# The opening of an attention and feed-forward kernel in one written order

## The chip, the cores and the metric

The kernel runs on one core of one Trainium2 chip. The metric is the device time of one execution in microseconds; the figure for a kernel is the median of its runs. The names of the engines are those of the profile: PE is TensorE, DVE is VectorE, ACT is ScalarE, POOL is GpSimd, and SP is the queue from which the kernel issues its DMAs.

## What is computed

An attention over 4 batches, 8 heads, 768 positions and 64 dimensions of a head, with a local window (96 positions) and 8 global keys, followed by a gated feed-forward part on 3072 tokens. Cut to what matters:

```python
scores = (1 / sqrt(D)) * q @ k.T
keep = is_global | is_local                     # pos < 8, or 0 <= rel < 96
scores = where(keep, scores - slopes * dist, -1e9)
a = softmax(scores)
x = reshape(a @ v)                              # 3072 x 512
h = ((x @ w1) * (x @ w2)) @ w3                  # w1, w2: 512 x 1024; w3: 1024 x 1024
return (h @ w_out).astype(float32)              # w_out: 1024 x 512
```

The four weights are float64 in memory.

## The kernel before

**The product of the two last weights.** Since nothing stands between `w3` and `w_out`, the kernel multiplies them once, at its start: the product, 1024 x 512, has eight row blocks f = 0 to 7 of 128 rows, and each is a sum over eight k of a matmul of a 128 x 128 block of `w3` (transposed, from `w3t`) with row block k of `w_out` (L96). `fold` does this.

**Converting the weights.** A float64 weight comes in pieces of 128 x 512 numbers (512 KB). `words` (L45) loads one piece as pairs of 32-bit words into a raw buffer, and three DVE operations (L53, L54, L55) shift and join the words into float32. There are 40 pieces: 8 of `w_out` (tile `wo`), 16 of `w3t` (tiles `t3_f_z`, two halves z of each row block f; the profile calls them `t`), and 16 of `w1` and `w2` (tile `t3s`). The pieces for the product take turns in four raw buffers `stage` (L82), those of `w1` and `w2` in two, `raws` (L132). In the text below t_f_z, o_k and w_k are these pieces, in that order.

**Two parts of a number.** Where PE is to multiply with nearly float32 accuracy, a matrix is split into a high part and a low part (`split`, L58): ACT copies x into a tile of the type float32r, and a subtraction gives x minus that copy. For the activations DVE subtracts; for `w1`, `w2` (L139) and for the product of the weights (L101) GpSimd does. `done` (L98) first copies a finished row block of the product from PSUM to `wf`, then splits `wf` into `wh` and `wl`.

**The steps.** The attention has 24 steps `s`; each takes two pairs of heads of a block of 256 queries. A step on PE has the values of the step before (L435, L437), the scores (L392), and four `flip`s, transposes of the probabilities (L423, L425). `softmax` (L395) has the fused bias, maximum and subtraction on DVE (L407), the exponential on ACT (L408), a sum and reciprocal on DVE (L409, L410), and the scaling, of one head of a pair on ACT (L413) and of the other on DVE (L414). The transposed probabilities are copied out of PSUM by ACT (L427). `split` at L482 takes a step's result into `xh` and `xl`, the input of the feed-forward part. `biases` makes the masks and distances; `bias` scales them for two heads.

**What sets the order.** The order on PE is written out (`manual_schedule`, L459); on the other engines and on SP a planner chooses. Feed-forward work (`run`, L142) and the product of the weights (`fold`, L86) are generators, cut into slices, which PE does between the flips: `SLICES` says how many stand ahead of each flip of a step. `fold` has 16 slices (L119: row blocks 2 to 7 in turn, after 0 and 1 together), so that with `FIRST` the steps 0 to 3 hold the product and one slice more, and the feed-forward part begins at the end of step 3. `ins` (L129) converts `w1` and `w2`, 1, 4, 4, 4 and 3 pieces ahead of the steps 0 to 4 (`INS`, L447).

PE's order on one step, as written:

```python
for m in range(STEP * NQ):
    slices(SLICES[s][m])
    phs.append(flip(*pairs(s)[m // NQ], m % NQ, prs[m // NQ]))
slices(SLICES[s][-1])
```

The product's accumulators are in the pool `ps_m` (two buffers), those of the values in `ps_v` (one), those of the flips in `ps_t` (one).

Of the kernel before, what the change touches and what calls it, by code (L numbers as in the profile page):

```python
# [20 lines left out]
P = 128  # L21
# [23 lines left out]
def words(nc, raw, dst, src):  # L45

    if src.dtype == F32:
        nc.sync.dma_start(out=dst, in_=src.bitcast(I32))
        return
    nc.sync.dma_start(out=raw, in_=src.bitcast(I32))  # L50
    w = raw.rearrange("p (n t) -> p n t", t=2)

    nc.vector.tensor_scalar(out=dst, in0=w[:, :, 1], scalar1=3, scalar2=0x3FFFFFF8, op0=ALU.logical_shift_left, op1=ALU.bitwise_and)  # L53
    nc.vector.scalar_tensor_tensor(out=dst, in0=w[:, :, 1], scalar=-0x40000000, in1=dst, op0=ALU.bitwise_and, op1=ALU.bitwise_or)  # L54
    nc.vector.scalar_tensor_tensor(out=dst, in0=w[:, :, 0], scalar=29, in1=dst, op0=ALU.logical_shift_right, op1=ALU.bitwise_or)  # L55


def split(nc, hi, lo, x, eng=None):  # L58

    nc.scalar.activation(hi, x, AF.Copy)  # L60
    (eng or nc.vector).tensor_tensor(out=lo, in0=x, in1=hi.bitcast(F32), op=ALU.subtract)  # L61


class FeedForward:
# [3 lines left out]
    def __init__(self, ctx, tc, w1, w2, w3t, w_out, out):  # L68
        self.nc = tc.nc
        self.src = (w1, w2)  # L70
        self.w3t, self.w_out, self.out = w3t, w_out, out
        self.wp = wp = ctx.enter_context(tc.tile_pool(name="wp", bufs=1))
        self.mp = ctx.enter_context(tc.tile_pool(name="mp", bufs=2))
        self.ps = ctx.enter_context(tc.tile_pool(name="ps_m", bufs=2, space=PSUM))
        self.w = [[wp.tile([P, NFC, NCC, P], F32R, name=f"w{n}{x}") for x in "hl"] for n in (1, 2)]
        self.wh, self.wl = (wp.tile([P, NFC, DO], F32R, name=n) for n in ("wh", "wl"))

        self.wo = self.mp.tile([P, NFC, DO], I32, tag="gh", bufs=1, name="wo")
        self.stage = self.mp.tile([P, 4, 2 * PC], I32, tag="gl", bufs=1, name="stage")
        self.turn = 0  # L80

    def staged(self, dst, src):  # L82
        words(self.nc, self.stage[:, self.turn % 4], dst, src)
        self.turn += 1

    def fold(self):  # L86
        nc = self.nc
        t3 = {}

        def piece(f, z):  # L90
            t3[f] = self.mp.tile([P, PC], I32, tag="ag"[z], name=f"t3_{f}_{z}")
            self.staged(t3[f], self.w3t[f, :, z * PC:(z + 1) * PC])

        def product(ps, f, k):
            z, i = divmod(k, HF)
            nc.tensor.matmul(ps, lhsT=t3[f][:, i * P:(i + 1) * P].bitcast(F32), rhs=self.wo[:, k].bitcast(F32), start=k == 0, stop=k == NFC - 1)  # L96

        def done(ps, f):  # L98
            full = self.mp.tile([P, DO], F32, tag="o", name=f"wf_{f}")
            nc.scalar.activation(full, ps, AF.Copy)  # L100
            split(nc, self.wh[:, f], self.wl[:, f], full, eng=nc.gpsimd)  # L101


        ps = [self.ps.tile([P, 512], F32, tag="m", name=f"w_{f}") for f in range(2)]
        for k in range(NFC):
            z, i = divmod(k, HF)
            if i == 0:
                piece(0, z)
            self.staged(self.wo[:, k], self.w_out[k])
            product(ps[0], 0, k)  # L110
            if i == 0:
                piece(1, z)
            product(ps[1], 1, k)
            if k == NFC - 1:
                for f in range(2):
                    done(ps[f], f)
            if k % 2:
                yield
        for f in range(2, NFC):  # L119
            ps = self.ps.tile([P, 512], F32, tag="m", name=f"w_{f}")  # L120
            for z in range(2):
                piece(f, z)
                for i in range(HF):
                    product(ps, f, HF * z + i)
                if z == 1:
                    done(ps, f)
                yield

    def ins(self, xp):  # L129
        nc = self.nc  # L130

        raws = xp.tile([P, 2, 2 * PC], I32, tag="xl", name="raws")  # L132
        t3s = xp.tile([P, 4, PC], I32, tag="xh", name="t3s")
        for k in range(2 * NFC):
            f, n = divmod(k, 2)
            t3 = t3s[:, k % 4]
            words(nc, raws[:, k % 2], t3, self.src[n][f])
            x = t3.bitcast(F32).rearrange("p (i m) -> p i m", i=NCC)
            split(nc, self.w[n][0][:, f], self.w[n][1][:, f], x, eng=nc.gpsimd)  # L139
            yield  # L140
# [42 lines left out]
def attention_moe(ctx: ExitStack, tc: tile.TileContext, qk, vx, w1, w2, w3t, w_out, ns, out):  # L183
# [3 lines left out]
    nt = cp.tile([P, 4], I32, name="nt")  # L187
    nc.sync.dma_start(out=nt, in_=ns.bitcast(I32).partition_broadcast(P))
    ident = cp.tile([P, P], F32, name="ident")
    make_identity(nc, ident)  # L190
    nf = cp.tile([P, 4], F32, name="nf")
    nc.vector.tensor_copy(out=nf, in_=nt)
    ff = FeedForward(ctx, tc, w1, w2, w3t, w_out, out)
    banded(tc, ff, nf, ident, qk, vx)

    okt = cp.tile([P, 6], F32, name="okt")
    for i, (c, s, op) in enumerate(((0, 0.0, ALU.is_ge), (0, float(GLB), ALU.is_le), (2, 1.0, ALU.is_ge), (2, float(WIN), ALU.is_le), (1, 0.0, ALU.is_equal), (3, 0.0, ALU.is_equal))):
        nc.vector.tensor_scalar(out=okt[:, i:i + 1], in0=nf[:, c:c + 1], scalar1=s, scalar2=None, op0=op)
    okm = cp.tile([P, 1], F32, name="okm")
    nc.vector.tensor_reduce(out=okm, in_=okt, axis=mybir.AxisListType.X, op=ALU.min)  # L200
    oki = cp.tile([P, 1], I32, name="oki")
    nc.vector.tensor_copy(out=oki, in_=okm)
# [113 lines left out]

@with_exitstack
def banded(ctx, tc, ff, nf, ident, qk, vx):
# [17 lines left out]
    def biases():  # L336
# [13 lines left out]
        nc.vector.tensor_scalar(out=loc, in0=rel, scalar1=0.0, scalar2=None, op0=ALU.is_ge)  # L350
        nc.vector.scalar_tensor_tensor(out=loc, in0=rel, scalar=nl, in1=loc, op0=ALU.is_lt, op1=ALU.mult)
# [21 lines left out]
    def load(c, hp):  # L373
        b, cb = divmod(c, NCB)
        k0 = 0 if cb else BW
        nw = 2 * NQ if cb else 2 * NQ - 1
        qr = ld.tile([P, QW], F32, tag="qr", name=f"qr_{c}_{hp}")
        vr = ld.tile([P, 2 * NQ, 2 * D], F32, tag="vr", bufs=2 * STEP, name=f"vr_{c}_{hp}")
        nc.sync.dma_start(out=qr[:, k0:], in_=qk[b, cb, hp, :, k0:])
        nc.sync.dma_start(out=vr[:, :nw], in_=vx[b, cb, hp, :, :nw])  # L380
        return qr, vr

    def scores(c, hp, t):
# [11 lines left out]
    def softmax(c, hp, ps):  # L395
# [4 lines left out]
        for j in range(NQ):  # L400
            first = c % NCB == 0 and j == 0
            w0 = BW if first else 0
            for u in range(2):
# [4 lines left out]
                nc.scalar.activation(pr[:, j, u, w0:], pr[:, j, u, w0:], AF.Exp, bias=m, scale=-1.0, accum_out=sm[:, j, u:u + 1])  # L408
        nc.vector.tensor_scalar(out=sm, in0=sm, scalar1=1e-9, scalar2=None, op0=ALU.add)  # L409
        nc.vector.reciprocal(out=sm, in_=sm)  # L410
        for j in range(NQ):
            w0 = BW if c % NCB == 0 and j == 0 else 0
            nc.scalar.activation(pr[:, j, 0, w0:], pr[:, j, 0, w0:], AF.Copy, scale=sm[:, j, 0:1])  # L413
            nc.vector.tensor_scalar(out=pr[:, j, 1, w0:], in0=pr[:, j, 1, w0:], scalar1=sm[:, j, 1:2], scalar2=None, op0=ALU.mult)  # L414
# [15 lines left out]
    def values(uu, c, hp, t, phs):  # L430
        for j, ph in enumerate(phs):
            first = c % NCB == 0 and j == 0
            for u in range(2):
                rows, o = slice(u * D, (u + 1) * D), uu[u * D:(u + 1) * D, j * P:(j + 1) * P]
                nc.tensor.matmul(o, lhsT=t[1][:, j, rows], rhs=ph[:, u, 0], start=True, stop=first)  # L435
                if not first:
                    nc.tensor.matmul(o, lhsT=t[1][:BW, 2 * NQ - 1 - j, rows], rhs=ph[:BW, u, 1], start=False, stop=True)  # L437
# [6 lines left out]

    FIRST = 1
    SLICES = [(2, 1, 1, 0, 0)] * 4 + [(5, 2, 2, 2, 1)] * (n - 4)
    INS = [1, 4, 4, 4, 3]  # L447
# [8 lines left out]
    work.append(ff.fold())  # L456
    more = ff.ins(xp)
    phs, vals = [], []
    with tc.manual_schedule(engines={mybir.EngineType.PE}):  # L459
        ts = [load(*pairs(0)[0])]  # L460
        slices(FIRST)
        dists = biases()
        ts += [load(*p) for p in pairs(0)[1:]]
        for s in range(n + 1):
            for _ in range(INS[s] if s < len(INS) else 0):
                next(more, None)
            if s < NP // STEP:
                for _, hp in pairs(s):
                    bias(hp, *dists)
            if s:  # L470
                c, h0 = pairs(s - 1)[0]
                if h0 == 0 and c % 2 == 0:
                    xs = [xp.tile([P, NCC, W], F32R, tag=tag, name=f"{tag}_{c}") for tag in ("xh", "xl")]
                xc = [x[:, :, c % 2 * T:][:, :, :T] for x in xs]
                uu = ps_v.tile([P, STEP, T], F32, tag="v", name=f"v_{c}_{h0}")
                for i, p in enumerate(pairs(s - 1)):
                    values(uu[:, i], *p, vals[i], phs[NQ * i:NQ * (i + 1)])
            if s < n:
                ps = [scores(*p, t) for p, t in zip(pairs(s), ts)]
            if s:  # L480
                hs = slice(h0, h0 + STEP)
                split(nc, xc[0][:, hs], xc[1][:, hs], uu)  # L482
# [61 lines left out]
```

## Time and profile before

| | us |
|---|---|
| median of 3 runs | 644.0 (643.03 to 644.11) |
| the profiled execution | 642.88 |
| its span, first to last instruction | 641.0 |
| PE busy in the span | 595.4 |
| ACT busy | 288.7 |
| DVE busy | 270.2 |
| POOL busy | 37.4 |

The span is what the views of the trace divide; the profiled execution's own time has 1.9 us around it. A row of a view of time gives the start, the length, the engine, the line, the operation, what is written and read, the count, and in brackets the idle time ahead of it with what ended it. A row of windows gives a stretch, its length, the busy time of PE, of PE's weight loads, of DVE, of ACT and of POOL with the number of instructions, then the granted clock of PE, the busy share of the DMA engines, and GB/s. A row of waits says who waited for whom, the total, how often, and the longest. A row of DMA issues ends with KB of one and the median time from issue to landing.

### The profile page before, as it was taken

What the parts mean: (1) busy time and instruction counts of PE and PEld (TensorE: products, weight loads), DVE (VectorE), ACT (ScalarE), POOL (GpSimd) and SP (SyncE); (2) the same over time, 40 slices, a digit from 0 to 9 for tenths busy, and PEclk for the clock granted to TensorE, in tenths of its full rate; (3) what the DMA queues carried; (4) which work ended last, traced back from release to release, by engine and by line L of the source; (5) the groups of instructions that cost most, each with busy time, mean ns of one, the idle gap of its engine ahead of it and who ended that gap; (6) DMA issues with size and microseconds to landing.
All of it is one profiled execution on the core that took longest, in us unless ns stands there. A gap on an engine that the chain in (4) does not pass through costs nothing.

```text
span 641.0 us, 9165 instructions
## 1 busy us (share of the span) xinstructions
PE 595.4 (93%) x3488; PEld 466.7 (73%) x3488; DVE 270.2 (42%) x839; ACT 288.7 (45%) x769; POOL 37.4 (6%) x34
## 2 busy tenths in 40 slices
PE   3678695999999999999999999999999999999996
PEld 1234444698898888888778888888888888888884
DVE  6999999234223333430444233334313442312210
ACT  0625364555345545643555355455525654522210
POOL 0033543200000000000000000000000000000000
PEclk9799797999999999999999999999999999999999
DMA  8768654102202210221122032101221220000001
GB/s 321 260 242 303 205 178 138 43 33 59 92 1 90 91 48 26 74 75 50 59 74 74 4 113 97 42 17 59 91 84 39 74 74 1 34 33 1 0 18 53
DMA packets 23237, 53.96 MB, mean 84 GB/s; under 512 B 2704, under 2 KB 4752, under 8 KB 23184
## 3 DMA queue, kind: packets, MB, share of 16 engines
q1 hardware_dynamic: 23184, 53.29, 25.0%
q8 instruction: 29, 0.48, 0.3%
q14 instruction: 24, 0.20, 0.1%
HBM read 46.99 MB, written 6.29 MB: 83 GB/s over the span
## 4 chain that ended last, share of the span: by engine, by line
PE 79%; DVE 12%; ACT 5%; issue 2%; DMA 2%; POOL 0%; SPq 0%; DVEq 0%; ACTq 0%
PE m L154 14%; PE m L156 13%; PE m L155 13%; PE o L171 7%; PE o L173 7%; PE o L172 7%; PE s L392 4%; PE v L435 4%; ACT pr L408 3%; PE t L423 3%; PE v L437 3%; PE t L425 3%; DVE t L54 2%; PE w L96 2%; DMA stage<-w3t 2%
## 5 line engine op out<-in xcount | busy, mean ns | idle before, releaser
L427 ACT ACTIVATE ph<-t 128x512 f32<-128x512 f32 (+1 forms) x96 | 53.8, 560 | 103.4 <-PE t L425 89.1
L408 ACT ACTIVATE pr<-pr,mx 128x232 f32<-128x232 f32 (+1 forms) x192 | 88.4, 462 | 24.6 <-DVE mx L407 24.6
L164 DVE TENSOR_TENSOR g<-m,a 128x512 f32<-128x512 f32 x48 | 33.1, 690 | 135.4 <-PE m L156 135.4
L154 PE MATMUL m<-xh,w1h 128*128 128x512 f32 (+1 forms) x224 | 85.2, 380 | 1.4 <-ACT a L161 1.4
L154 PE MATMUL m<-xh,w2h 128*128 128x512 f32 (+1 forms) x224 | 83.0, 370 | 0.0
L155 PE MATMUL m<-xl,w1h 128*128 128x512 f32 (+1 forms) x224 | 80.8, 361 | 0.0
L156 PE MATMUL m<-xh,w2l 128*128 128x512 f32 (+1 forms) x224 | 80.8, 361 | 0.0
L155 PE MATMUL m<-xl,w2h 128*128 128x512 f32 (+1 forms) x224 | 80.8, 361 | 0.0
L156 PE MATMUL m<-xh,w1l 128*128 128x512 f32 (+1 forms) x224 | 80.8, 361 | 0.0
L171 PE MATMUL o<-wh,gh 128*128 128x512 f32 x192 | 78.7, 410 | 1.5 <-ACT a L161 1.5
L96 PE MATMUL w<-wo,t 128*128 128x512 f32 x128 | 63.2, 639 | 17.3 <-DVE wo L55 16.9
L173 PE MATMUL o<-wh,gl 128*128 128x512 f32 x192 | 75.2, 392 | 0.0
L172 PE MATMUL o<-wl,gh 128*128 128x512 f32 x192 | 75.2, 391 | 0.0
L61 DVE TENSOR_TENSOR xl<-v,xh 128x512 fp32r<-128x512 f32 x24 | 16.6, 690 | 132.7 <-ACT xh L60 132.7
L423 PE MATMUL t<-ident,pr 128*128 128x128 f32 x192 | 46.3, 277 | 16.4 <-ACT ph L427 16.2
L60 ACT ACTIVATE gh<-g 128x512 fp32r<-128x512 f32 x48 | 30.3, 631 | 65.6 <-DVE g L164 65.6
L96 PEld LDWEIGHTS w<-wo,t 128*128 128x128 f32 x128 | 24.2, 201 | 48.4 <-issue 22.9
L407 DVE CUSTOM_DVE_ANT_0 pr<-s,biasw 128x232 f32<-128x232 f32 x160 | 54.7, 394 | 0.0
L154 PEld LDWEIGHTS m<-xh,w1h 128*128 128x128 f32 x224 | 42.1, 188 | 12.4 <-issue 4.8
L61 DVE TENSOR_TENSOR gl<-g,gh 128x512 fp32r<-128x512 f32 x48 | 33.2, 692 | 34.0 <-ACT gh L60 34.0
L156 PEld LDWEIGHTS m<-xh,w1l 128*128 128x128 f32 x224 | 42.0, 188 | 7.4
L156 PEld LDWEIGHTS m<-xh,w2l 128*128 128x128 f32 x224 | 42.0, 188 | 7.4
(72 smaller groups left out, 891.3 us busy)
## 6 DMA issues: line engine op xcount, KB each, us to landing
qr<-qk SPq DMA_DIRECT2D x32, 312.0 KB, 3.8
stage<-w3t SPq DMA_DIRECT2D x16, 512.0 KB, 5.5
raws<-w SPq DMA_DIRECT2D x16, 512.0 KB, 3.6
vr<-vx SPq DMA_DIRECT2D x32, 256.0 KB, 2.9
out_dram<-ot SPq DMA_DIRECT2D x24, 256.0 KB, 2.0
qr<-qk SPq DMA_DIRECT2D x16, 260.0 KB, 3.2
stage<-w_out SPq DMA_DIRECT2D x8, 512.0 KB, 5.0
vr<-vx SPq DMA_DIRECT2D x16, 192.0 KB, 3.1
```

What stands on the lines that cost most here:

```text
L61: (eng or nc.vector).tensor_tensor(out=lo, in0=x, in1=hi.bitcast(F32), op=ALU.subtract)
L96: nc.tensor.matmul(ps, lhsT=t3[f][:, i * P:(i + 1) * P].bitcast(F32), rhs=self.wo[:, k].bitcast(F32), start=k == 0, stop=k == NFC - 1)
L154: nc.tensor.matmul(ps[:, z], lhsT=mh, rhs=xh[:, i], start=i == 0, stop=False)
L155: nc.tensor.matmul(ps[:, z], lhsT=mh, rhs=xl[:, i], start=False, stop=False)
L156: nc.tensor.matmul(ps[:, z], lhsT=ml, rhs=xh[:, i], start=False, stop=i == NCC - 1)
L171: nc.tensor.matmul(ps, lhsT=gh[:, f, ts], rhs=self.wh[:, f], start=f == 0, stop=False)
L172: nc.tensor.matmul(ps, lhsT=gh[:, f, ts], rhs=self.wl[:, f], start=False, stop=False)
L173: nc.tensor.matmul(ps, lhsT=gl[:, f, ts], rhs=self.wh[:, f], start=False, stop=f == NFC - 1)
L407: nc.vector.tensor_tensor_reduce(out=pr[:, j, u, w0:], in0=ps[u][:, j, w0:UW], in1=bias, scale=-SCALE, scalar=3.0e38, op0=ALU.add, op1=ALU ...
L408: nc.scalar.activation(pr[:, j, u, w0:], pr[:, j, u, w0:], AF.Exp, bias=m, scale=-1.0, accum_out=sm[:, j, u:u + 1])
L423: nc.tensor.transpose(pt[:, u, 0], pr[:, j, u, BW:UW], ident)
L427: nc.scalar.activation(ph[:, :, :nk], pt[:, :, :nk], AF.Copy)
```

## The change

- `words` becomes `convert`, which takes one or two pieces: both loads are issued, then each of the three DVE operations is done for both before the next one.
- `weights` names the pieces of one such call. The w3t pieces go round the tags a, g, a, g, o, o; the raw buffers of the product's pieces are eight (four of `stage`, four in the tags xh and xl) up to the last piece of `w_out`, four afterwards.
- The product is made of row blocks 0, 1 and 2 at once (the third in the pool of the values), then 3 beside step 0, 4 and 5 beside step 1, 6 and 7 beside step 2. `fold` issues the matmuls of one block, and ACT copies a finished block from PSUM straight to `wh`; `low` subtracts from PSUM, on DVE.
- The subtractions for `w1` and `w2` are on DVE too, one call of `weights` after the copy (`late`, `lows`). GpSimd has none any more.
- `first_steps` writes out the steps 0 to 3 with all conversions, for PE, DVE and SP; ACT is left to the planner. Its loads of the queries and keys and of the values are apart (`load`, `load_values`) and come after ten and fourteen pieces. The load of the two numbers `nt` comes after two pieces, the masks are in two parts, and the biases of all heads are made at once.
- In every step the rows of both head pairs (`rows`) come ahead of the sums and scalings (`softmax`). In the steps 0 to 3 ACT scales both heads of a pair.
- The slices of the steps 3 to 7 are 10, 10, 10, 9 and 9 where there were 1 (in step 3) and 12; from step 8 on they are as before. The feed-forward part begins in step 3, ahead of its flips.
- The test whether the two numbers fit the banded form (`fits`) stands behind step 3.

```diff
-def words(nc, raw, dst, src):
+def convert(nc, pieces):
+    for dst, raw, src in pieces:
+        nc.sync.dma_start(out=dst if src.dtype == F32 else raw, in_=src.bitcast(I32))
+    pieces = [(dst, raw.rearrange("p (n t) -> p n t", t=2)) for dst, raw, src in pieces if src.dtype != F32]
+    for dst, w in pieces:
+        nc.vector.tensor_scalar(out=dst, in0=w[:, :, 1], scalar1=3, scalar2=0x3FFFFFF8, op0=ALU.logical_shift_left, op1=ALU.bitwise_and)
+    for dst, w in pieces:
+        nc.vector.scalar_tensor_tensor(out=dst, in0=w[:, :, 1], scalar=-0x40000000, in1=dst, op0=ALU.bitwise_and, op1=ALU.bitwise_or)
+    for dst, w in pieces:
+        nc.vector.scalar_tensor_tensor(out=dst, in0=w[:, :, 0], scalar=29, in1=dst, op0=ALU.logical_shift_right, op1=ALU.bitwise_or)
...
+    def weights(self, *names):
+        pieces, fresh = [], []
+        for kind, *at in names:
+            if kind == "w":
+                f, n = divmod(at[0], 2)
+                dst, raw, src = self.t3s[:, at[0] % 4], self.raws[:, at[0] % 2], self.src[n][f]
+                fresh.append((n, f, dst.bitcast(F32).rearrange("p (i m) -> p i m", i=NCC)))
...
+        convert(self.nc, pieces)
+        self.lows()
+        for n, f, x in fresh:
+            hi, lo = (w[:, f] for w in self.w[n])
+            self.nc.scalar.activation(hi, x, AF.Copy)
+            self.late.append((lo, x, hi))
...
+    def lows(self):
+        for lo, x, hi in self.late:
+            self.nc.vector.tensor_tensor(out=lo, in0=x, in1=hi.bitcast(F32), op=ALU.subtract)
+        self.late = []
...
+            if k == NFC - 1:
+                nc.scalar.activation(self.wh[:, f], ps, AF.Copy)
+    def low(self, f):
+        self.nc.vector.tensor_tensor(out=self.wl[:, f], in0=self.prod[f], in1=self.wh[:, f].bitcast(F32), op=ALU.subtract)
...
+    def first_steps():
+        ff.more_stages(xp)
+        masks = biases()
+        next(masks)
+        ff.weights(("t", 0, 0))
+        ff.weights(("o", 0))
+        nc.sync.dma_start(out=nt, in_=ns.bitcast(I32).partition_broadcast(P))
+        ff.fold(0, 0)
+        ff.weights(("t", 1, 0), ("t", 2, 0))
+        ff.fold(1, 0)
+        ff.fold(2, 0, pool=(ps_v, "v"))
+        ff.weights(("o", 1), ("o", 2))
...
+        for _ in masks:
+            pass
+        ff.weights(("o", 3), ("t", 0, 1))
...
+        ff.weights(("t", 1, 1), ("t", 2, 1))
+        loads(0, vals=False)
+        ff.weights(("o", 4), ("o", 5))
+        ps = visit(0)
...
+        ff.weights(("o", 6), ("o", 7))
+        loads(0, keys=False)
+        prs = all_rows(0, ps)
+        for f in range(3):
+            ff.fold(f, 6, 7)
+        w = (("w", k) for k in range(2 * NFC))
+        ff.weights(("t", 3, 0), next(w))
+        for s in range(3):
+            fs = (3,) if s == 0 else (2 * s + 2, 2 * s + 3)
+            if s:
+                prs = all_rows(s, visit(s))
+                ff.fold(fs[0], *range(NFC))
+                ff.weights(("t", fs[1], 1), next(w))
+                ff.low(fs[0] - 1)
+            for p, r in zip(pairs(s), prs):
+                softmax(*p, *r, nc.scalar)
+            loads(s + 1)
+            if s:
+                ff.low(fs[0])
+            else:
+                ff.low(0)
+                ff.weights(("t", 3, 1), next(w))
+                ff.low(1)
+                ff.low(2)
+            for m in range(STEP * NQ):
+                ff.fold(fs[-1], 2 * m, 2 * m + 1)
+                turn(s, m, prs)
+                if m and fs[-1] == NFC - 1:
+                    ff.weights(next(w))
+                elif m:
+                    ff.weights(("t", fs[-1] + 1 + (m == 3), (m - 1) % 2), next(w))
+        s = 3
+        prs = all_rows(s, visit(s))
+        ff.low(NFC - 1)
+        ff.weights(next(w), next(w))
+        slices(2)
+        for p, r in zip(pairs(s), prs):
+            softmax(*p, *r, nc.scalar)
+        loads(s + 1)
+        ff.weights(next(w))
+        slices(SLICES[s][0] - 2)
+        ff.lows()
+        for m in range(STEP * NQ):
+            turn(s, m, prs)
+            slices(SLICES[s][m + 1])
+        fits(nc, ff.mp, nf, oki)
+    SLICES = [()] * 3 + [(4, 2, 2, 1, 1)] * 3 + [(4, 2, 1, 1, 1)] * 2 + [(5, 2, 2, 2, 1)] * (n - 8)
     with tc.manual_schedule(engines={mybir.EngineType.PE}):
+        with tc.manual_schedule(engines={mybir.EngineType.DVE, mybir.EngineType.SP}):
+            first_steps()
+        for s in range(4, n + 1):
+            rs = all_rows(s, visit(s))
+            for p, r in zip(pairs(s), rs):
+                softmax(*p, *r, nc.vector)
...
```

`visit(s)` issues the values of the step before, the scores of step s and the split of the values, as the loop did before; `turn` is one flip.

More of the change, by code (lines that the diff above doesn't have):

```diff
@@ L129, in ins @@
[L129 to L140, printed above, removed]
+        gl = self.mp.tile([P, 4, 2 * PC], I32, tag="gl", bufs=1, name="stage")
@@ new lines, in __init__, with more_stages, next @@
+        self.stage = [gl[:, i] for i in range(4)]
+        self.t3, self.prod, self.late, self.turn = {}, {}, [], [0, 0, 0]
+    def more_stages(self, xp):
+        self.first = [x[:, i] for x in (xp.tile([P, 2, 2 * PC], I32, tag=t, name=f"stage_{t}") for t in ("xh", "xl")) for i in range(2)]
+        self.t3s = xp.tile([P, 4, PC], I32, tag="xh", name="t3s")
+        self.raws = xp.tile([P, 2, 2 * PC], I32, tag="xl", name="raws")
+    def next(self, ring, slots):
+        self.turn[ring] += 1
+        return slots[(self.turn[ring] - 1) % len(slots)]
@@ new lines, in weights @@
+    def weights(self, *names):
[5 more added lines that the diff above has]
+                fresh.append((n, f, dst.bitcast(F32).rearrange("p (i m) -> p i m", i=NCC)))
+            elif kind == "o":
+                dst, src = self.wo[:, at[0]], self.w_out[at[0]]
+            else:
+                f, z = at
+                dst = self.mp.tile([P, PC], I32, tag=self.next(0, "agagoo"), name=f"t3_{f}_{z}")
+                src = self.w3t[f, :, z * PC:(z + 1) * PC]
+                self.t3[f, z] = dst
+            if kind != "w":
+                raw = self.next(1, self.stage + self.first)
+            pieces.append((dst, raw, src))
+        convert(self.nc, pieces)
[4 more added lines that the diff above has]
+            self.late.append((lo, x, hi))
+        if names[0] == ("o", NFC - 2):
+            self.first = []
@@ new lines, in lows, with fold @@
+    def lows(self):
+        for lo, x, hi in self.late:
+            self.nc.vector.tensor_tensor(out=lo, in0=x, in1=hi.bitcast(F32), op=ALU.subtract)
+        self.late = []
+    def fold(self, f, *ks, pool=None):
+        nc = self.nc
+        if f not in self.prod:
+            pool, tag = pool or (self.ps, "m")
+            self.prod[f] = pool.tile([P, 512], F32, tag=tag, name=f"w_{f}")
+        ps = self.prod[f]
+        for k in ks:
+            z, i = divmod(k, HF)
+            nc.tensor.matmul(ps, lhsT=self.t3[f, z][:, i * P:(i + 1) * P].bitcast(F32), rhs=self.wo[:, k].bitcast(F32), start=k == 0, stop=k == NFC - 1)
+            if k == NFC - 1:
+                nc.scalar.activation(self.wh[:, f], ps, AF.Copy)
@@ L314, in dense, with fits, banded @@
             pass
+def fits(nc, mp, nf, oki):
+    okt = mp.tile([P, DO], F32, tag="o", name="okt")[:, :8]
+    for i, (c, s, op) in enumerate(((0, 0.0, ALU.is_ge), (0, float(GLB), ALU.is_le), (2, 1.0, ALU.is_ge), (2, float(WIN), ALU.is_le), (1, 0.0, ALU.is_equal), (3, 0.0, ALU.is_equal))):
+        nc.vector.tensor_scalar(out=okt[:, i:i + 1], in0=nf[:, c:c + 1], scalar1=s, scalar2=None, op0=op)
+    nc.vector.tensor_reduce(out=okt[:, 6:7], in_=okt[:, :6], axis=mybir.AxisListType.X, op=ALU.min)
+    nc.vector.tensor_copy(out=oki, in_=okt[:, 6:7])
 @with_exitstack
-def banded(ctx, tc, ff, nf, ident, qk, vx):
+def banded(ctx, tc, ff, ns, nt, nf, oki, ident, qk, vx):
     nc = tc.nc
@@ L361, in biases @@
             nc.vector.tensor_tensor(out=d, in0=d, in1=m, op=ALU.add)
-        return dist0, dist
-    def bias(hp, dist0, dist):
-        for h in (2 * hp, 2 * hp + 1):
+        for h in range(H):
             sl = -SLOPES[h] / SCALE
@@ L443, in banded @@
     work = []
[L445 to L447 removed]
+    qrs, vrs, phs, xs = {}, {}, {}, {}
     def slices(k):
@@ L454, in slices @@
                 k -= 1
-    work.append(ff.fold())
-    more = ff.ins(xp)
-    phs, vals = [], []
-    with tc.manual_schedule(engines={mybir.EngineType.PE}):
[L460 to L482, printed above, removed]
-                if h0 + STEP == NP and c < 2:
-                    work.append(ff.run(c, *xc, c * T, T))
-                elif h0 + STEP == NP and c % 2:
-                    work.append(ff.run(c, *xs, (c - 1) * T, W))
-            if s < n:
-                prs = [softmax(*p, x) for p, x in zip(pairs(s), ps)]
-                vals = ts
-                if s + 1 < n:
-                    ts = [load(*p) for p in pairs(s + 1)]
-                phs = []
-                for m in range(STEP * NQ):
-                    slices(SLICES[s][m])
-                    phs.append(flip(*pairs(s)[m // NQ], m % NQ, prs[m // NQ]))
-                slices(SLICES[s][-1])
-            else:
-                slices(10 ** 6)
@@ new lines, in loads, with visit @@
+    def loads(s, keys=True, vals=True):
+        if s < n and keys:
+            qrs[s] = [load(*p) for p in pairs(s)]
+        if s < n and vals:
+            vrs[s] = [load_values(*p) for p in pairs(s)]
+    def visit(s):
+        if s:
+            c, h0 = pairs(s - 1)[0]
+            if h0 == 0 and c % 2 == 0:
+                xs[c // 2] = [xp.tile([P, NCC, W], F32R, tag=tag, name=f"{tag}_{c}") for tag in ("xh", "xl")]
+            uu = ps_v.tile([P, STEP, T], F32, tag="v", name=f"v_{c}_{h0}")
+            for i, p in enumerate(pairs(s - 1)):
+                values(uu[:, i], *p, vrs[s - 1][i], phs[s - 1][NQ * i:NQ * (i + 1)])
+        ps = [scores(*p, t) for p, t in zip(pairs(s), qrs[s])] if s < n else []
+        if s:
+            x2 = xs[c // 2]
+            xc = [x[:, :, c % 2 * T:][:, :, :T] for x in x2]
+            split(nc, *(x[:, h0:h0 + STEP] for x in xc), uu)
+            if h0 + STEP == NP and c < 2:
+                work.append(ff.run(c, *xc, c * T, T))
+            elif h0 + STEP == NP and c % 2:
+                work.append(ff.run(c, *x2, (c - 1) * T, W))
+        return ps
@@ new lines, in banded @@
+    SLICES = [()] * 3 + [(4, 2, 2, 1, 1)] * 3 + [(4, 2, 1, 1, 1)] * 2 + [(5, 2, 2, 2, 1)] * (n - 8)
+    with tc.manual_schedule(engines={mybir.EngineType.PE}):
+        with tc.manual_schedule(engines={mybir.EngineType.DVE, mybir.EngineType.SP}):
[4 more added lines that the diff above has]
+                softmax(*p, *r, nc.vector)
+            if s == n:
+                break
+            loads(s + 1)
+            for m in range(STEP * NQ):
+                slices(SLICES[s][m])
+                turn(s, m, rs)
+            slices(SLICES[s][-1])
+        slices(10 ** 6)
```

111 lines of the change are left out of this document (41 added, 70 removed).

## The prediction

> **What bounds the kernel now.** First the page (busy shares, 40 slices of 16 us), then windows, what TensorE (PE) waited for, and VectorE's (DVE's) order of time.
>
> ```profile
> PE 595.4 (93%) x3488; PEld 466.7 (73%) x3488; DVE 270.2 (42%) x839; ACT 288.7 (45%) x769; POOL 37.4 (6%) x34
> ...
> DVE  6999999234223333430444233334313442312210
> ...
> PEclk9799797999999999999999999999999999999999
> ```
> ```profile
> 0.00:119.84 119.84, 84.19 (x320) 43.21 (x321) 105.74 (x242) 51.04 (x144) 36.09 (x33) 0.91 0.64 220
> 119.84:641.00 521.16, 511.18 (x3171) 423.52 (x3169) 164.41 (x597) 237.63 (x626) 1.26 (x1) 1.00 0.17 53
> 119.84:200.00 80.16, 76.55 (x671) 70.78 (x669) 28.07 (x113) 40.94 (x116) 1.26 (x1) 1.00 0.20 60
> ```
> ```profile
> PE w L96 <- DVE wo L55: 16.9, 4, 10.2
> PE t L423 <- ACT ph L427: 16.2, 4, 7.7
> ```
> ```profile
> 119.84 0.37 PE L154 MATMUL m<-xh,w1h 128*128 128x256 f32 x1
> ```
>
> PE is the bound of the whole (93%), yet until 119.84 us, where the first feed-forward matmul starts, it is busy 84.2 us and DVE 105.7 (the third and fifth numbers of a windows row). After that PE is busy 511.2 of 521.2. So the opening is DVE's: it converts 40 weight pieces by three operations each (L53 to L55), and PE waits for them. Only the opening can be shortened; what follows is PE's.
>
> **The change, part by part.** First the price of a conversion, from DVE's order of time: a pair, a piece alone, and one beside GpSimd (POOL).
>
> ```profile
> 62.33 0.41 DVE L53 TENSOR_SCALAR t3s<-raws 128x512 int32<-128x512 int32 x1
> 63.00 0.68 DVE L54 SCALAR_TENSOR_TENSOR t3s<-raws,t3s 128x512 int32<-128x512 int32 x1
> 63.60 0.68 DVE L54 SCALAR_TENSOR_TENSOR t<-stage,t 128x512 int32<-128x512 int32 x1
> ...
> 65.41 0.43 DVE L53 TENSOR_SCALAR t<-stage 128x512 int32<-128x512 int32 x1
> ...
> 99.62 0.42 DVE L53 TENSOR_SCALAR t3s<-raws 128x512 int32<-128x512 int32 x1
> ...
> 101.41 0.42 DVE L53 TENSOR_SCALAR t3s<-raws 128x512 int32<-128x512 int32 x1
> ```
> ```profile
> 40.13 3.13 POOL L61 TENSOR_TENSOR wl<-wf,wh 128x512 fp32r<-128x512 f32 x2
> 40.38 1.75 DVE L54 SCALAR_TENSOR_TENSOR t3s<-raws,t3s 128x512 int32<-128x512 int32 x1
> 42.06 1.75 DVE L54 SCALAR_TENSOR_TENSOR t<-stage,t 128x512 int32<-128x512 int32 x1
> ```
> ```profile
> 0.00:119.84 119.84, 23.68 (x40) 0.91 0.64 220
> ...
> 0.00:119.84 119.84, 33.74 (x40) 0.91 0.64 220
> ...
> 0.00:119.84 119.84, 28.56 (x40) 0.91 0.64 220
> ```
>
> A pair takes 65.41 - 62.33 = 3.08 us, one alone 101.41 - 99.62 = 1.79. Beside a POOL subtraction the 0.68 us operation takes 1.75. The last fence gives L53, L54 and L55: 85.98 us for 40 pieces, where undisturbed bars (0.42, 0.68, 0.68) would give 71.2. With no subtraction on POOL about 14.8 us go. In return DVE takes over 24 subtractions.
>
> ```profile
> 53.25 0.68 DVE L61 TENSOR_TENSOR xl<-v,xh 128x512 fp32r<-128x512 f32 x1
> 53.85 0.28 DVE L407 CUSTOM_DVE_ANT_0 pr<-s,bias 128x128 f32<-128x128 f32 x1
> ...
> 56.03 0.17 DVE L409 TENSOR_SCALAR sm<-sm 128x4 f32<-128x4 f32 x1
> ```
> ```profile
> 12.25 0.45 DVE L351 SCALAR_TENSOR_TENSOR loc<-rel,nf,loc 128x232 f32<-128x232 f32 x1
> ```
> ```profile
> 0.75 0.39 SPq L188 DMA_DIRECT2D nt<-ns  x1
> ...
> 2.13 0.43 SPq L50 DMA_DIRECT2D stage<-w3t  x1
> ...
> 6.39 0.43 DVE L53 TENSOR_SCALAR t<-stage 128x512 int32<-128x512 int32 x1 [1.71 <-DMA stage<-w3t]
> ```
>
> A subtraction takes 0.60 (53.25 to 53.85, reading PSUM as `low` will), eight score rows 2.18 in a step of a first block (steps 0 and 1) and, estimated, 2.6 in steps 2 and 3, where all are wide. The sum and reciprocal of a step: 0.8, estimated from the 0.17 us operation, four of them with gaps. The second part of the masks is twelve operations of at most 0.45: 3.0, estimated. The first piece is issued at 2.13 and used at 6.39; issued first, at 0.75, it is there at 5.0 (bounds 4.0 and 6.4: without the two attention loads ahead of it, or no earlier).
>
> Now DVE in its written order, from 5.0. Up to the first rows: 2 pieces alone 3.6, six pairs 18.5, masks 3.0, rows 2.2: 32.3. Step 0: five pairs 15.4, sums 0.8, seven subtractions 4.2 (three products, four weights): 52.7. Step 1: four pairs 12.3, four weight and two product subtractions and xl 4.2, rows 2.2, sums 0.8: 72.2. Step 2: one pair 3.1, three pieces alone 5.4, seven subtractions 4.2, rows 2.6, sums 0.8: 88.3. Step 3 up to its sums: xl, `low`(7), one pair, one weight subtraction, rows, sums: 3.1 + 1.8 + 2.6 + 0.8 = 8.3: 96.6. With two scalings on ScalarE (ACT) the first transpose of step 3 can go at 97.4, if DVE never waits.
>
> It will wait where it needs PE. The prices:
>
> ```profile
> 86.41 0.27 PE L423 MATMUL t<-ident,pr 128*128 128x128 f32 x1
> ...
> 86.84 3.60 PE L96 MATMUL w<-wo,t 128*128 128x512 f32 x8
> ```
> ```profile
> 301.86 0.45 PE L435 MATMUL v<-ph,vr 128*64 128x128 f32 x4
> ...
> 303.82 1.50 PE L392 MATMUL s<-qr 64*128 64x128 f32 x16
> ...
> 305.25 0.50 PE L154 MATMUL m<-xh,w1h 128*128 128x512 f32 x1
> ...
> 308.16 0.39 PE L154 MATMUL m<-xh,w2h 128*128 128x512 f32 x1
> ```
> ```profile
> 72.66 0.47 PE L423 MATMUL t<-ident,pr 128*128 128x128 f32 x1 [5.65 <-ACT ph L427]
> ...
> 102.69 0.47 PE L423 MATMUL t<-ident,pr 128*128 128x128 f32 x1 [7.67 <-ACT ph L427]
> ```
>
> A flip is 0.43, a product matmul 0.45, a step's values 1.96, two slices of feed-forward 2.91, so 1.45 each. After 5.65 and 7.67 idle us a transpose takes 0.47 instead of 0.27: the clock has dropped. Steps 0 and 1 give PE long cover: its loop of four flips and eight product matmuls is 5.3 us at full clock, some 9 if it starts cold, and DVE has 11 us of pairs beside it. In step 2 the cover is three pieces alone with their subtractions, 7.2 us. The loop starts about 82 (sums at 80.4, then ACT), ends near 91, values and the ACT copy at 93; DVE comes at 88.3. I take 4.5 us of wait there (bounds 0 with the clock full, 8 with all of it at half), and 0.6 where t_1_1's buffer still holds `dist` until 16 bias activations have read it. The Trainium skill ("TensorE: Matmul & The Clock Gate", The HAM clock gate) says that PE falls to half clock after about 3.4 us idle; the rows at 5.65 and 7.67 agree, and by that section the 5 us between products 6 and 7 here would start the loop cold, as it does in the sum.
>
> So the first flip of step 3 comes at 102.5. PE then stands where it stood before at 119.84, ahead by four feed-forward slices (5.8) and behind by two flips (0.9). Left: 521.2 - 4.9 = 516.3. Span 102.5 + 516.3 = 618.8. The profiled execution was 642.88 for a span of 641.0, so 1.9 around it, and it lies 1.1 under the median of 644.0: 621.8, said as **622**.
>
> What costs nothing, and by what cover. The scaling of every second head moves to ACT for four steps: 16 operations, beside an ACT that is busy 51 of 119.8 us. `fits` moves from the start (free, DVE waiting for data) to the end of step 3, under PE's slices; uncovered, 1 us. nt's load goes behind two pieces on SP, the attention loads behind ten; the masks' second half and the scores come later than those land. Slices per step become 10, 10, 10, 9, 9 in steps 3 to 7 where there was 1, then 12 each: 48 against 49 by the end of step 7, so only the order of the same PE work differs. The eight copies to wf vanish from ACT, which was not late. Three products hold three accumulators, the third in the values' buffer, free once `low`(2) has run, long before values.
>
> The Trainium skill ("VectorE: DVE Perf Modes", The DRAIN you can't avoid) speaks against the pairs: the next operation starts only when the pipe is empty, whatever the order. The rows at 63.00 and 63.60 start 0.60 apart with bars of 0.68, so here it doesn't hold for independent neighbours.
>
> **Rivals.**
>
> *DMA decides (slower).* The input weights have two raw buffers, and SP issues in written order: piece k is issued when k-2 is converted.
>
> ```profile
> raws<-w SPq DMA_DIRECT2D x16, 512.0 KB, 3.6
> ...
> vr<-vx SPq DMA_DIRECT2D x4, 192.0 KB, 7.3
> ```
>
> With landing time L one such piece comes every (L + 3.1)/2 us where it is one of a pair, every (L + 1.8)/2 where it stands alone. At 3.6 that is 3.4 and 2.7, where DVE itself needs 3.7 and 2.4 with the subtraction: hidden but for 1 us, which the wait of step 2 takes in. At 7.3 it is 5.2 and 4.5: 8 x 1.5 + 3 x 2.1 = 18, less that wait of 4.5: 636. At 8.8 the loss is 26.5 less 4.5, and the time that of before: from there on it is slower. I price it at L = 9.5, 8 x 2.6 + 3 x 3.3 = 31 less 4.5: 648. For it: the DMA share of 0.64 in the windows row of the opening (second number from the end), and SP held up by order; against: 3.6 was the median for these very loads in that traffic.
>
> *The steps' chains decide.* DVE in fixed order waits at each of three step starts for flips, copies, values and scores, which a planner could cover with pieces. With 6 us at each, about the 5.65 and 7.67 seen: 18 instead of 4.5, so 635.
>
> *No relief.* The slow conversions would stay without POOL: 14.8 more, 637. Against: the long bars lie beside POOL's.
>
> *No gain from pairs*, as an emptying pipe would have it: 17 x (2 x 1.79 - 3.08) = 8.5 more, 630. The DRAIN section above is that rule.
>
> *Better.* No wait at step 2, the first piece at 4.0, and some of the 3.6 us that PE idles between 119.84 and 200 gone too: 622 - 4.5 - 1 - 3, 613.
>
> **How the numbers follow.** Forecast 622 (617 to 628): 54%. Chains 635: 18%. Better 613: 16%. DMA 648: 6%. No pair gain 630: 3%. No relief 637: 3%. A measurement here tells about 0.2% (1.3 us) from no change. Faster 0.93 (a hundredth of the chains goes to same), same 0.01, slower 0.06. Range 611 to 637: it leaves out the DMA case and the tails of chains and better.
>
> **What would show it.** L53 to L55 at 0.34, 0.60, 0.60 from start to start with no bar of 1.4 or more; DVE's last product conversion near 79 instead of 97; the first feed-forward matmul near 95, the first flip of step 3 near 102; PE's full stretch beginning there. Wrong if DVE idles over 10 us for SP's loads or for scores, if PE stays at half clock through steps 0 to 2, or if PE has new gaps after step 3 because both pairs' rows come ahead of the scalings: there 4 to 5 slices (5.8 to 7.3 us) stand between scores and the first flip.

## The result and the profile after

The changed kernel takes 622.23 us (median of 4 runs, 621.55 to 622.91), the kernel before, run beside it, 643.51. The ratio is 0.9671, 95% interval 0.9653 to 0.9689: faster by 21 us. The forecast was 622, in a range of 611 to 637. The profiled execution took 622.35 us for a span of 620.6.

The page of the changed kernel, with the rows that answer to those shown of before (busy shares, then 40 slices of 15.5 us):

```profile
PE 593.9 (96%) x3488; PEld 463.4 (75%) x3488; DVE 260.0 (42%) x847; ACT 288.6 (47%) x777; POOL 1.3 (0%) x10
...
DVE  5999988533434335303434313532232442212200
...
PEclk9999899999999999999999999999999999999998
```

PE's own work is the same (593.9 us against 595.4); the span got shorter around it. DVE's full slices (a 9) end two slices earlier, and PE's clock falls in one slice of the opening where it fell in three. The opening in windows of the changed kernel (length, PE, PE's weight loads, DVE, ACT, POOL, clock, DMA share, GB/s), up to the first flip of step 3 and behind it:

```profile
0.00:104.73 104.73, 85.40 (x360) 45.33 (x360) 91.37 (x236) 50.32 (x146) 1.32 (x10) 0.97 0.70 250
104.73:620.60 515.87, 508.48 (x3128) 418.06 (x3128) 168.66 (x611) 238.27 (x632) 0.00 (x0) 1.00 0.17 54
```

What PE waited for in the first 105 us, longest in total first (total, times, longest):

```profile
PE w L139 <- DVE wo L57: 11.0, 2, 8.5
PE w L139 <- DVE wl L144: 3.4, 1, 3.4
PE w L139 <- DVE t L57: 2.8, 1, 2.8
PE t L438 <- ACT pr L427: 1.6, 1, 1.6
PE t L438 <- ACT ph L442: 0.3, 1, 0.3
```

The waits for flips' copies (`ph`), 16.2 us before, are nearly gone; those for converted weights remain (13.8 us, 17.3 before). The 3.4 us for `wl` are new: product 5 needs the accumulator of product 3, which `low`(3) still has to read. Behind this wait lies the one slice with a lowered clock (0.8 from 62 to 78 us): the same four instructions take 3.46 us there, and 1.88 in the next row.

```profile
63.92 3.46 PE L139 MATMUL w<-wo,t 128*128 128x512 f32 x4 [3.41 <-DVE wl L144]
...
67.44 1.88 PE L139 MATMUL w<-wo,t 128*128 128x512 f32 x4
```

What DVE waited for in the first 105 us:

```profile
DVE t L53 <- DMA stage<-w3t: 4.7, 3, 2.5
DVE wl L144 <- ACT wh L141: 2.0, 1, 2.0
DVE rel L352 <- POOL it L350: 1.7, 1, 1.7
DVE xl L63 <- ACT xh L62: 1.7, 2, 1.1
DVE t3s L53 <- DMA raws<-w: 1.4, 2, 0.9
DVE t L53 <- ACT bias L370: 0.5, 1, 0.5
```

And the busy time of DVE in the three lines of a conversion (L53, L55 and L57 of the changed kernel, by windows up to 112 us; all 40 pieces are in it):

```profile
sum 112.00, DVE 15.58; mean DVE 15.58
...
sum 112.00, DVE 26.03; mean DVE 26.03
...
sum 112.00, DVE 26.01; mean DVE 26.01
```

That is 67.6 us where it was 86.0, and no more than the 71.2 of undisturbed bars: neighbouring bars overlap, and the busy time counts the overlap once.

### The profile page after: what moved, and what is told of

The parts are those of the page before. It is cut to its first block, busy times and chain, and to the rows that moved or that the text cites. A ratio compares the mean times of both kernels' runs of the same rounds, so it can differ in the third digit from the quotient of the medians.

```text
span 620.6 us, 9123 instructions
## 1 busy us (share of the span) xinstructions
PE 593.9 (96%) x3488; PEld 463.4 (75%) x3488; DVE 260.0 (42%) x847; ACT 288.6 (47%) x777; POOL 1.3 (0%) x10
## 4 chain that ended last, share of the span: by engine, by line
PE 71%; DVE 12%; ACT 10%; DMA 5%; issue 1%; SPq 0%; ACTq 0%; DVEq 0%
PE m L158 12%; PE m L160 11%; PE m L159 11%; PE o L175 7%; PE o L177 7%; PE o L176 7%; ACT pr L415 5%; PE v L450 4%; PE t L438 3%; PE s L399 3%; PE v L452 3%; PE t L440 3%; ACT pr L427 2%; DMA stage<-w3t 2%; DMA raws<-w 2%; DVE pr L414 2%
## 5 line engine op out<-in xcount | busy, mean ns | idle before, releaser
L139 PE MATMUL w<-wo,t 128*128 128x512 f32 x128 | 65.0, 655 | 17.3 <-DVE wo L57 11.0
L414 DVE CUSTOM_DVE_ANT_0 pr<-s,biasw 128x232 f32<-128x232 f32 x160 | 53.4, 394 | 0.0
L158 PEld LDWEIGHTS m<-xh,w2h 128*128 128x128 f32 x224 | 42.2, 188 | 7.9 <-ACT a L165 0.6
```

Source lines behind the costliest of these rows:

```text
L139: nc.tensor.matmul(ps, lhsT=self.t3[f, z][:, i * P:(i + 1) * P].bitcast(F32), rhs=self.wo[:, k].bitcast(F32), start=k == 0, stop=k == NFC - 1)
L158: nc.tensor.matmul(ps[:, z], lhsT=mh, rhs=xh[:, i], start=i == 0, stop=False)
L414: nc.vector.tensor_tensor_reduce(out=pr[:, j, u, w0:], in0=ps[u][:, j, w0:UW], in1=bias, scale=-SCALE, scalar=3.0e38, op0=ALU.add, op1=ALU ...
```

## The experiments

Each run also stood beside runs of the kernel before on the same chip (643.1 to 643.7 us median).

**One piece after the other.**

```diff
     for dst, w in pieces:
         nc.vector.tensor_scalar(out=dst, in0=w[:, :, 1], ...)
-    for dst, w in pieces:
         nc.vector.scalar_tensor_tensor(out=dst, in0=w[:, :, 1], ...)
-    for dst, w in pieces:
         nc.vector.scalar_tensor_tensor(out=dst, in0=w[:, :, 0], ...)
```

> The changed kernel, with the three DVE operations done for one piece after the other; both loads of a call are still issued first. If DVE's sum sets the end of the opening (my theory): 17 pairs up to the first flip of step 3 lose 0.5 us each, 8.5 us, less some 1 to 2 us of DVE's waits that this fills: 629 us (627 to 631). If the written order is what matters and DVE has room (rival): within 2 us of 622.

Measured 628.65 us, ratio 0.9772 (0.9755 to 0.9788): 6.4 us more than the changed kernel. The pairs are worth most of the 8.5 us that the gaps between dependent operations add up to, and in the changed kernel DVE's work does reach the end.

**The input weights' subtractions on GpSimd again.**

```diff
-            self.nc.vector.tensor_tensor(out=lo, in0=x, in1=hi.bitcast(F32), op=ALU.subtract)
+            self.nc.gpsimd.tensor_tensor(out=lo, in0=x, in1=hi.bitcast(F32), op=ALU.subtract)
```

> The changed kernel, with the 16 subtractions of the input weights on GpSimd again (the eight of the product stay on DVE, since they read PSUM). My theory, DVE's sum: 13 of them stand before the first flip of step 3, so DVE loses 7.8 us of work and gains 13 blockings of some 0.7 us (14.8 us for 22 before the change): about +1, 621 to 626 us. Rival, that GpSimd's blocking was the main loss of before: 632 us or more.

Measured 625.53 us, ratio 0.9719 (0.9693 to 0.9744): 3.3 us more: within the range expected, though the sum behind it said about 1. By lines (L53, L55, L57, up to 112 us) the conversions grow from 67.6 to 74.3 us:

```profile
sum 112.00, DVE 18.81; mean DVE 18.81
...
sum 112.00, DVE 28.18; mean DVE 28.18
...
sum 112.00, DVE 27.32; mean DVE 27.32
```

DVE loses 10.9 us of subtractions, and still the first feed-forward matmul comes later (102.57 us, 97.31 in the changed kernel): beside the conversions, the small sums (L420) grow from 1.2 to 4.5 us.

**The kernel before, with its subtractions on DVE.**

```diff
-            split(nc, self.wh[:, f], self.wl[:, f], full, eng=nc.gpsimd)
+            split(nc, self.wh[:, f], self.wl[:, f], full)
...
-            split(nc, self.w[n][0][:, f], self.w[n][1][:, f], x, eng=nc.gpsimd)
+            split(nc, self.w[n][0][:, f], self.w[n][1][:, f], x)
```

> The kernel before, with its 24 subtractions on DVE instead of GpSimd and nothing else changed. My theory, DVE's sum: 14.8 us of slow conversions and some 4 us of slow scalings go, 22 x 0.6 = 13.2 us come: 5 us less, 636 to 641 us. Rival, that GpSimd's blocking was the main loss: about 628 us. Rival, that only the order counts: 643 us.

Measured 628.98 us, ratio 0.9777 (0.9753 to 0.9801): 14.5 us faster than before by this edit alone. That is the figure of the rival that GpSimd's holds were the main loss (a hold: an operation of DVE that takes longer beside one of GpSimd), not mine. The conversions fell to 69.5 us and the scalings (L414) from 9.6 to 5.7; the 24 subtractions came on top. That the subtractions only finished late on GpSimd is not the reason: in the kernel before none of the listed waits of PE or DVE up to 120 us ended on a result of GpSimd. What PE waited for in this run, in the first 130 us:

```profile
PE w L96 <- DVE wo L55: 18.3, 4, 10.3
PE w L96 <- DVE t L55: 4.2, 3, 3.5
PE t L423 <- ACT ph L427: 3.5, 4, 1.8
```

The wait for flips' copies fell from 16.2 to 3.5 us, and the first feed-forward matmul starts at 105.16 instead of 119.84.

**DVE and SP left to the planner.**

```diff
-        with tc.manual_schedule(engines={mybir.EngineType.DVE, mybir.EngineType.SP}):
-            first_steps()
+        first_steps()
```

> The changed kernel, with DVE and SP in the opening left to the planner; PE's order stays as written. If DVE's sum alone counts: 622 to 626 us, since the operations are the same ones. If the written order on DVE and SP is what brings the gain (rival): 632 to 643 us.

Measured 620.52 us, ratio 0.9647 (0.9628 to 0.9666). It lies 1.7 us under the changed kernel, whose interval (0.9653 to 0.9689) it overlaps: the written order on DVE and SP brings nothing that can be measured.

**A new theory: ACT's queue.** Why did the subtractions on GpSimd cost so much before? In the kernel before, on GpSimd, DVE and ACT in order of time:

```profile
95.31 1.71 POOL L61 TENSOR_TENSOR wl<-wf,wh 128x512 fp32r<-128x512 f32 x1
96.98 1.44 POOL L61 TENSOR_TENSOR w1l<-t3s,w1h 128x512 fp32r<-128x512 f32 x1
```
```profile
95.82 1.49 DVE L53 TENSOR_SCALAR t<-stage 128x512 int32<-128x512 int32 x1
97.34 1.63 DVE L54 SCALAR_TENSOR_TENSOR t<-stage,t 128x512 int32<-128x512 int32 x1
```
```profile
101.53 0.63 ACT L60 ACTIVATE w2h<-t3s 128x512 fp32r<-128x512 f32 x1 [4.96 <-DVE t3s L55]
102.06 0.58 ACT L427 ACTIVATE ph<-t 128x512 f32<-128x512 f32 x1
```

GpSimd holds up two operations of DVE (1.49 and 1.63 us, 0.42 and 0.68 undisturbed); ACT has stood idle for a late conversion (4.96 us) to make a weight's copy; the copy of a flip that PE had done by 95 comes after it, at 102.06; and PE's next flip, shown in the prediction, starts at 102.69 after 7.67 us idle, with a lowered clock (0.79 granted from 96 to 112 us). So a hold of a microsecond or two may grow where copies of several chains stand in one queue. Two edits tried to break this and keep GpSimd's work.

```diff
-            split(nc, self.w[n][0][:, f], self.w[n][1][:, f], x, eng=nc.gpsimd)
+            late.append((self.w[n][0][:, f], self.w[n][1][:, f], t3.bitcast(F32).rearrange("p (i m) -> p i m", i=NCC)))
+            if k:
+                split(nc, *late[k - 1], eng=nc.gpsimd)
...
```

> The kernel before, subtractions still on GpSimd, but the copy (ACT) and the subtraction of an input weight are written one piece later than its conversion, so that in ACT's queue the copies of flips come ahead of them. New theory, ACT's queue: GpSimd holds up a conversion, the copy of that piece waits at the head of ACT's in-order queue, the flip's copy stands behind it, and PE waits (16.2 us in four waits, and some 3 us of lowered clock). Then PE's wait falls to 6 us or less and the time to 630 to 636 us. If only DVE's sum counts (rival): 641 to 645 us, since DVE's operations and GpSimd's are the same ones.

Measured 642.22 us, ratio 0.9981 (0.9965 to 0.9997). This decides nothing: the planner put the copies of weights ahead of the flips' copies all the same, and PE's wait is as long as before:

```profile
PE t L427 <- ACT ph L431: 16.5, 6, 7.7
```

The second writes ACT's order out (steps 0 to 3), with all bias activations in step 0, and makes the weights' copies and subtractions at the end of a step:

```diff
+        act.enter_context(tc.manual_schedule(engines={mybir.EngineType.Activation}))
...
+            if s == 4:
+                ff.flush()
+                act.close()
...
                 slices(SLICES[s][-1])
+                ff.flush()
```

> The kernel before, subtractions still on GpSimd, with ACT's order of the steps 0 to 3 written out: the copies of the input weights (and their subtractions) come behind a step's flips, not between them, and all bias activations come in step 0. The edit before this one left copies ahead of the flips' copies, and PE's wait for them did not fall (16.5 us). Theory, ACT's queue: now no flip's copy stands behind a weight's copy; PE's wait for them falls under 6 us and the time to 630 to 636 us, though GpSimd holds up as many conversions. Rival, the slow conversions themselves set the end: 641 us or more.

Measured 650.71 us, ratio 1.0112 (1.0086 to 1.0138): slower. What PE waited for in the first 135 us, then DVE, then PE behind that:

```profile
PE w L97 <- DVE wo L55: 15.0, 3, 10.3
PE t L429 <- ACT pr L419: 10.5, 3, 6.6
PE t L429 <- ACT ph L433: 4.0, 6, 1.3
```
```profile
DVE t3s L53 <- POOL w2l L61: 18.3, 3, 11.6
```
```profile
117.15 0.36 PE L160 MATMUL m<-xh,w1h 128*128 128x256 f32 x1
...
138.17 0.58 PE L160 MATMUL m<-xh,w1h 128*128 128x256 f32 x1 [9.28 <-ACT a L167]
```

The wait for flips' copies fell to 4.0 us as meant. But the conversions of the next step now wait 18.3 us for GpSimd to free their buffers, and PE waits 10.5 us for scalings. The opening even ended 2.7 us earlier: the first feed-forward matmul starts at 117.15, before at 119.84. The loss comes behind it, in one wait of 9.28 us that the edit itself made: ACT's copy `a` of a feed-forward result (L167) now stands behind two late copies of weights and behind step 4's exponentials and scalings. One wait was traded for others, so ACT's queue is neither shown nor excluded as the way by which GpSimd's holds reach the end.

**The kernel before without subtractions.**

```diff
-            split(nc, self.w[n][0][:, f], self.w[n][1][:, f], x, eng=nc.gpsimd)
+            nc.scalar.activation(self.w[n][0][:, f], x, AF.Copy)
...
```

The product's eight subtractions are left out in the same way, and each low part is the tile of the high part.

> The kernel before, with no low part of the weights at all: the 24 subtractions are left out, and the matmuls that read a low part read the high part, so PE's work is the same. Beside the run with 24 subtractions on DVE (629.0 us): if those cost DVE's sum in full, 0.6 us each, 614 to 617 us; if they lie off the path that sets the end, 626 to 629 us.

Measured 628.05 us, ratio 0.9761 (0.9723 to 0.9799), against 628.98 (0.9753 to 0.9801) with the 24 subtractions on DVE. So on DVE they cost some 1 us there (by the intervals 4 at most), although they are 24 x 0.6 = 14.4 us of its work, while on GpSimd they cost some 15. The work was not on the path; the holds were. DVE's waits in the run without them, longest first, in the first 130 us:

```profile
DVE xl L61 <- ACT xh L60: 11.4, 1, 11.4
DVE t L53 <- DMA stage<-w3t: 6.8, 4, 2.3
```

The 11.4 us are no wait on the way to the end of the opening. Free of subtractions, DVE has all 40 conversions done at 97.6 us (107.8 with them) and then stands idle from 100.1 to 111.5. PE's first feed-forward matmul comes no earlier for it: at 105.48 us, and at 105.16 with the subtractions. In this order something else than DVE's sum sets the end, once the holds are gone.

**Two operations of three.**

```diff
-    for dst, w in pieces:
-        nc.vector.scalar_tensor_tensor(out=dst, in0=w[:, :, 0], scalar=29, in1=dst, ...)
```

> The changed kernel, with the last of the three DVE operations of a conversion left out (the lowest three bits of the weights are lost). 39 x 0.6 = 23 us of DVE's work before the first flip of step 3 go. If DVE's sum sets the end of the opening: 599 to 606 us. If loads, PE or ACT stand close behind DVE (rival): 612 us or more, with DVE idle for them.

Measured 611.76 us, ratio 0.9519 (0.9484 to 0.9554): 10.5 us for 23 us of DVE's work. DVE's waits in it up to 105 us:

```profile
DVE t3s L53 <- DMA raws<-w: 6.7, 5, 2.5
DVE t L53 <- DMA stage<-w3t: 5.9, 3, 2.5
DVE wl L142 <- ACT wh L139: 5.8, 3, 3.1
DVE xl L61 <- ACT xh L60: 3.6, 2, 3.0
```

Both sides hold in part. In the changed kernel DVE's sum does set the end of the opening, but loads and the chain through PE and ACT stand close behind it. The first flip of step 3 comes at 93.42 us here; up to it the rows of those two kinds add up to 19.5 us (2.5 of the 6.7 us for w come later), to 9.8 in the changed kernel.

**Two row blocks at once.**

```diff
-        ff.weights(("t", 1, 0), ("t", 2, 0))
+        ff.weights(("t", 1, 0), ("o", 1))
...
+        ff.weights(("t", 2, 0), ("t", 2, 1))
+        ff.low(0)
+        ff.fold(2, *range(NFC))
         ff.weights(("t", 3, 0), next(w))
```

> The changed kernel, with two row blocks of the product at once instead of three: t_2_0 and t_2_1 come after w_out's last pieces, and block 2 is made in one go ahead of block 3, in step 0. DVE's operations are the same. If DVE's sum and waits set the end: 621 to 624 us. If the third block is what fills PE's early waits (rival): PE has 8 matmuls (3.6 us) more to do later, 625 to 627 us.

Measured 620.39 us, ratio 0.9649 (0.9624 to 0.9673). That is 0.6 us below the range for the sum, and not the 625 of the rival: the third block brings nothing.

**Versions to go on with.** First the masks and `low`(6) moved to where DVE waited:

```diff
         ff.weights(("t", 0, 0))
+        nc.sync.dma_start(out=nt, in_=ns.bitcast(I32).partition_broadcast(P))
         ff.weights(("o", 0))
-        nc.sync.dma_start(out=nt, in_=ns.bitcast(I32).partition_broadcast(P))
+        for _ in masks:
+            pass
...
                     ff.weights(next(w))
+                    if m == 1:
+                        ff.low(fs[0])
```

> The changed kernel, with the second part of the masks ahead of the pair t_1_0, t_2_0, where DVE waited 2.3 us for loads (the load of nt one place earlier), and with low(6) after the first weight that follows it, where DVE waited 2.0 us for ACT's copy. If DVE's sum and waits set the end: 2.2 + 0.5 + 2.0 us less, 617 to 619 us. If PE's or ACT's chain takes over (rival): 621 to 623 us.

Measured 620.33 us, ratio 0.9644 (0.9618 to 0.9671), between the two: 1.9 us less than the changed kernel by medians, with intervals that overlap. The wait at `low` is gone, but another of 3.2 us for `xh` came. Then the same with the planner on DVE and SP:

> The masks and low(6) moved as in the run of 620.3 us, and DVE and SP of the opening left to the planner as in the run of 620.5 us. If the two gains add: 617 to 619 us. If the planner already moves such operations by itself (rival): 620 to 621 us.

Measured 617.65 us, ratio 0.9605 (0.9585 to 0.9625), 5 runs. The interval lies below that of the changed kernel, so this version beats it; it overlaps that of the run before it (0.9618 to 0.9671). And, in the written order again, the moved operations with step 3's second head scaled on DVE:

```diff
-            softmax(*p, *r, nc.scalar)
+            softmax(*p, *r, nc.vector)
```

> The masks and low(6) moved as in the run of 620.3 us, and in step 3 the second head of a pair scaled on DVE again, where PE waited 1.5 us for ACT's scalings. If that wait is the path: 618.5 to 620 us. If DVE's four operations of 0.3 us take it back (rival): 620 to 622 us.

Measured 620.90 us, ratio 0.9660 (0.9639 to 0.9681): no gain.

## Why the prediction was right

**The time.** The prediction put the first flip of step 3 at 102.5 us and the rest at 516.3. Measured:

```profile
97.31 0.39 PE L158 MATMUL m<-xh,w1h 128*128 128x256 f32 x1
...
104.73 0.33 PE L438 MATMUL t<-ident,pr 128*128 128x128 f32 x1 [1.55 <-ACT pr L427]
```

The flip comes at 104.73, and 515.9 us follow. The opening was 2.2 us too short and the rest 0.4 too long; the time around the span and the distance to the median, taken from before, were 1.4 too much together (622.23 is 1.6 over the span, 3.0 were added). That these errors have opposite signs is luck: the total looks better than its terms.

**DVE's steps.** DVE started at 4.81 (5.0). It ended the first rows at 35.6 (32.3), step 0 at 56.8 (52.7), step 1 at 76.0 (72.2), step 2 at 95.1 (88.3). Nearly all of the lag is waits that the sum left out until its end or did not have: 2.3 us for the second and third w3t pieces, 0.5 for the bias activations (0.6 taken), 1.4 for the raw buffers, 2.0 for ACT's copy at `low`(6), and 0.6 for `xh`. The mask operations took 3.6 us (3.0).

**The mis-sized term.** For step 2 the sum had 4.5 us of wait at `xl`, with a loop on PE that starts cold, at a lowered clock; there were 1.15. The clock stayed full, as a window of the changed kernel shows (1.00, third number from the end):

```profile
80.00:96.00 16.00, 15.65 (x78) 8.32 (x78) 12.39 (x25) 10.63 (x27) 0.00 (x0) 1.00 0.51 171
```

The reason lies in a price. The prediction took 0.45 us for a product matmul, from a row of x8. But `fold` writes 64 matmuls (eight blocks, eight k) and the page counts 128 instructions: one matmul of the code is two, 0.9 us, and a whole block takes 7.13, not 3.6.

```profile
53.38 7.13 PE L139 MATMUL w<-wo,t 128*128 128x512 f32 x16
...
77.06 9.12 PE L139 MATMUL w<-wo,t 128*128 128x512 f32 x20
```

The second row is product 6 and the start of product 7, without a gap: the 5 us of idle time in which the clock was to fall did not exist. The loop of flips and product matmuls, put at 5.3 us at full clock and some 9 cold, comes to 4 x 0.43 + 8 x 0.9 = 8.9 at full clock. So its length was right by luck, with two errors that cancel. DVE came late to it as well (95.1 us, not 88.3), by the 2.0 us at `low`(6) and the early loads above all, and so waited only 1.15. All of DVE's waits from its first conversion to its rows of step 3 add up to 7.9 us where the sum had 5.1; that covers the 2.2 us by which the flip comes late.

**GpSimd.** The prediction set 14.8 us of slow conversions that go against 24 subtractions that come, 14.4 us, as a trade within DVE's sum. By this trade the move alone would gain next to nothing (with the scalings, some 5 us, as was expected of that run), and the rest was left to the other parts of the change. This was the wrong attribution. By the run of the kernel before with this one edit, the move alone is 14.5 of the 21 us; and by the run without any subtraction, the ones that came cost about 1 us there. The slow conversions and scalings were on the path, the subtractions fitted in where DVE would have waited. In the changed kernel, where DVE's sum is closer to the path, the same choice for 16 of them is worth 3.3 us.

**The pairs.** 8.5 us had been set for no gain from pairs; one after the other costs 6.4. The emptying pipe of the Trainium skill ("VectorE: DVE Perf Modes", The DRAIN you can't avoid) does not make order indifferent here: the run differs in nothing but the order of the same operations. That section also names an exception, a next operation that is not held starts earlier, which the prediction left out.

**The rivals.** DMA did not decide: landing of the input weights was 3.6 us again (page after, raws). The steps' chains did not: they were priced at 18 us of DVE waiting at three step starts, and its waits for `xh` there are 1.7, for scores none; with the planner in place of the written order the time is the same. The signs of being wrong did not come either: DVE idles 6.1 us for SP's loads, PE's clock is 0.97 over the opening, no single conversion bar is over 0.7, and behind the flip PE idles 7.4 us, where before it idled 10.0 behind 119.84. Better than forecast was in reach, but by another order (617.65).

**What stays open.** Which part of the change gives the 6.8 us between 628.98 and 622.23. It is not the third block, and not the written order of DVE and SP. The rows of PE's waits show where it lies: 18.3 us for pieces of `w_out` in that run, 11.0 in the changed kernel, while its other waits in the opening add up alike (7.7 and 8.3). Which edit shortens that wait is not shown. The scalings on ACT alone, the feed-forward slices in step 3 and the product ending a step earlier were not tried one by one. And whether GpSimd's holds reached the end through ACT's queue.

## What to carry to other kernels

Price an operation that holds up another engine by what it holds up, not by its own length or by a trade of sums: 24 subtractions were worth 14.5 us when moved from a mostly idle engine to the busiest one of the stretch. Test the smallest edit of a large change by itself; here two arguments of two calls held about two thirds of the gain of a rewrite. Where two chained operations on one engine have independent neighbours, put those between them: 6.4 us for 17 pairs.

## What the runs showed that was not expected

The busiest engine of a stretch (DVE, 105.7 of 119.8 us before) took 14.4 us more work at a cost of about 1 us, since time was left once GpSimd's holds had gone: it is busy 94.7 of 105.2 us in the run with all subtractions on DVE (fifth number), and 84.8 in the run without any.

```profile
0.00:105.17 105.17, 80.90 (x321) 40.26 (x321) 94.74 (x261) 50.83 (x143) 1.32 (x10) 0.95 0.72 251
```

And a planner that orders DVE and SP by itself did no worse than an order written by hand with every wait in view, and, with two operations moved, better than the changed kernel (617.65 against 622.23 us).
